# Running sum of key features: adding DMAs into DRAM from GpSimd's queue in place of VectorE additions in SBUF

## The chip, the cores and the metric

The kernel runs on one core of one Trainium2 chip. A core has five engines with a queue of instructions each: TensorE (PE) for matrix products, VectorE (DVE) and ScalarE (ACT) for element-wise work, GpSimd (POOL) for element-wise work beside them, and SyncE (SP), which here issues the transfers between DRAM and the core's memory (SBUF). Engines work in parallel and in the order of their own queue; they wait for each other through semaphores. The metric is the time of one execution on the device in microseconds, as the median of several runs.

## The reference, cut to what matters

The input `x` (2048 tokens of 1024 features) is normalised; an attention block A and a gated block B are computed of it, and the result is `x + A * silu(B)`. The change touches only a part of A:

```python
qkv = (x @ wqkv) ...                       # 32 heads of 32 features
pk = einsum("bhsd,hdf->bhsf", k, w_phi)
phi_k = concat([softmax(pk), softmax(-pk)], -1)     # 64 features per head and token
kv = einsum("bhsf,bhsd->bhfd", phi_k, v)   # sum over tokens
z  = einsum("bhsf->bhf", phi_k)            # sum over tokens
num = einsum("bhqf,bhfd->bhqd", phi_q, kv)
den = einsum("bhqf,bhf->bhq", phi_q, z) + 1e-6
o = num / den
```

`z`, the sum of the key features over all 2048 tokens, is what is accumulated in another way.

## The kernel before, in words

**Matrix products.** Large products are done by Strassen-like recombination into seven block products, named B11, T2, T3, B21, T1, T4 and B22. Each float32 operand is split into a high and a low part (`split`: line 130 on ScalarE makes the high part, line 131 on VectorE the low part), and `mm3` (lines 135 to 137) makes three matmuls of the parts. Several block products share a PSUM bank: B21 adds on top of B11, T4 on top of T3, B22 on top of T1, and between the two the bank is read into SBUF ("evacuated"). For the gated block these evacuations are line 1069 (B11, ScalarE), 1071 (T2), 1073 (T3), and 1079 to 1088 for the blocks that end a result; line 1089 multiplies a gate on GpSimd. In this stage one block is 4 x 3 = 12 matmuls.

**Stages.** The tokens are handled in two chunks of 1024. For each chunk come the projections V, K and Q, then the products with the gate and up weights (28 units of 7 blocks). After both chunks come the product with the down weights and the attention's second half. During chunk 0's gated stage and all of chunk 1, side work is mixed in as "background" tasks, one at a time: `background(anchor)` issues the next task from a list, to follow a given instruction. In chunk 1's gated stage one is issued every six blocks, and a second list (weight sums on GpSimd, `wd_sums`, lines 571 to 578) every fourteen.

**The task of the change.** `k_task(hb, t)` handles one tile of 128 tokens and one half `hb` of the heads: 16 tiles for each of two halves, 32 tasks. It loads raw keys and values (lines 463 and 464), makes the features (`features`, lines 446 to 454: maxima and minima, two subtractions at lines 449 and 450 that write the buffer `e_k`, the exponential at line 451 on ScalarE, sums and reciprocals), scales `e_k` in place (line 467), splits `e_k` and the values for TensorE (lines 130 and 131), and adds `e_k` (128 x 1024, 512 KB) to `zacc` (line 474 copies in the first tile, line 476 adds in the others). `e_k` is one buffer, slot 53, which all tasks use in turn; `zacc` is slot 54. The products of the task's features and values (line 486) are issued on TensorE with the next background task.

After the 16 tiles of a half, three more tasks follow: `kv_sum` and `kv_blocks`, which put the products together, and `z_broadcast` (line 521 on), which splits `zacc`, multiplies it by a matrix of ones so that each partition has the sum over all 128, and stores that to DRAM (`zb_d`).

**What sets the order.** Outside the first and last stages the order of each engine's queue is made at build time by a scheduler that simulates the program and places every instruction where it thinks it is ready; the anchors bound it from one side. Nothing reorders on the chip: an instruction that waits holds its engine's queue. SP issues nearly every transfer, among them the weight loads `w<-ws_d` (line 388), up to eight 512 KB slots ahead of their use. GpSimd issues none.

Of the kernel before, what the change touches and what calls it, by code (L numbers as in the profile page):

```python
# [10 lines left out]
F32 = mybir.dt.float32  # L11
F32R = mybir.dt.float32r
AF = mybir.ActivationFunctionType
ALU = mybir.AluOpType
# [4 lines left out]
P = 128  # L19
# [8 lines left out]
HB = 512  # L28
# [21 lines left out]
def hedgehog_glu_kernel(  # L50
# [12 lines left out]
    nc = tc.nc  # L63
# [4 lines left out]
    dram = ctx.enter_context(tc.tile_pool(name="dram", bufs=1, space=DRAM))  # L68
# [9 lines left out]
    xo_d = dram.tile([7, P, 4, HB], F32, name="xo_d")  # L78
    e_d = dram.tile([TT, 2, P, 2 * HB], F32, name="e_d")
    r_d = dram.tile([CTT, 2, P, 32], F32, name="r_d")  # L80
    zb_d = dram.tile([2, P, 2 * HB], F32, name="zb_d")
    kvbd_d = dram.tile([2, P, 2 * HB], F32, name="kvbd_d")
    ws_d = dram.tile([2 * NJ, 4, P, 2 * HB], F32, name="ws_d")
# [30 lines left out]
    def whole(i):  # L114
        return slots[i].rearrange("p a n -> p (a n)")
# [4 lines left out]
    def run(i, n):  # L120

        name, k = where[i]
        return blocks[name][0][:, k:k + n]

    def pair(i):
        return slots[i][:, 0], slots[i][:, 1]

    def split(o, src):

        nc.scalar.copy(o[0], src)  # L130
        return nc.vector.tensor_sub(o[1], src, o[0].bitcast(F32))  # L131
# [308 lines left out]
    def features(name, p, e):  # L440

        nh = HB // DH
        st = small.tile([P, 4, nh], F32, name=f"st{name}", tag="st", bufs=2)
        pv = p.rearrange("p (h d) -> p h d", d=DH)
        mx, mn = st[:, 0], st[:, 1]
        nc.vector.tensor_reduce(mx, pv, axis=AX.X, op=ALU.max)
        nc.vector.tensor_reduce(mn, pv, axis=AX.X, op=ALU.min)
        ev = e.rearrange("p (h t d) -> p h t d", t=2, d=DH)
        nc.vector.tensor_tensor(ev[:, :, 0], pv, mx[:, :, None].to_broadcast([P, nh, DH]), op=ALU.subtract)  # L449
        nc.vector.tensor_tensor(ev[:, :, 1], mn[:, :, None].to_broadcast([P, nh, DH]), pv, op=ALU.subtract)  # L450
        nc.scalar.activation(e, e, AF.Exp)  # L451
        s2, r2 = [st[:, a:a + 2].rearrange("p t h -> p (t h)") for a in (2, 0)]
        nc.vector.tensor_reduce(s2, e.rearrange("p (g d) -> p g d", d=DH), axis=AX.X, op=ALU.add)  # L453
        nc.vector.reciprocal(r2, s2)
        return r2
# [3 lines left out]
    e_k, zacc = whole(53), whole(54)  # L459
    kvb = banks[4:]  # L460

    def k_task(hb, t):
        nc.sync.dma_start(kraw, qkv_d[K, t, hb])
        nc.sync.dma_start(vraw, qkv_d[V, t, hb])
        r = features(f"k{t}{hb}", kraw, e_k)
        e3 = e_k.rearrange("p (g d) -> p g d", d=DH)
        nc.vector.tensor_mul(e3, e3, r[:, :, None].to_broadcast([P, 32, DH]))  # L467

        ph, v = [o.rearrange("p (g a f) -> p g a f", g=8, a=2)
                 for o in (run(36, 2).rearrange("p a b n -> p (a b n)"), whole(38))]  # L470
        split((ph[:, :, 0], ph[:, :, 1]), e_k.rearrange("p (g f) -> p g f", g=8))
        split((v[:, :, 0], v[:, :, 1]), vraw.rearrange("p (g f) -> p g f", g=8))
        if t == 0:
            nc.vector.tensor_copy(zacc, e_k)
        else:
            nc.vector.tensor_add(zacc, zacc, e_k)
        kv_due.append((t, ph, v))

    kv_due = deque()
# [40 lines left out]

    def z_broadcast(hb):

        for i in range(2):
            z = zacc[:, i * HB:(i + 1) * HB]
            a = pair(38)
            split(a, z)
            nc.tensor.matmul(kvb[i], ones, a[0], start=True, stop=False)
            nc.tensor.matmul(kvb[i], ones, a[1], start=False, stop=True)
            nc.scalar.copy(z, kvb[i])
        nc.sync.dma_start(zb_d[hb], zacc)  # L530
# [469 lines left out]
    for hb in range(2):  # L1000
        bg.extend([lambda hb=hb, t=t: k_task(hb, t) for t in range(TT)])
        bg.extend([lambda hb=hb, f=f: f(hb) for f in (kv_sum, kv_blocks, z_broadcast)])
# [162 lines left out]
    for n, (i, j, cs) in enumerate(dsteps):  # L1165
# [24 lines left out]
        if n and n * 32 // 78 > (n - 1) * 32 // 78 and late:  # L1190
            t, hb = late.pop(0)
# [193 lines left out]
```

## Time and profile before

| what | value |
|---|---|
| runs | 2380.21, 2378.32, 2374.84 us; median 2378.32 us |
| profiled execution, first to last instruction | 2376.2 us; the page gives no time outside it |
| TensorE busy | 2361.1 us (99%), granted clock 1.000 |
| VectorE busy | 1778.2 us (75%) |
| ScalarE busy | 1022.0 us (43%) |
| GpSimd busy | 959.8 us (40%) |
| DMA | 600.49 MB, mean 253 GB/s |

The page lists busy time by engine, a picture of the span in 40 slices, DMA queues, the chain of work that ended last, and groups of instructions by line with their count, busy time, mean duration and the idle time ahead of them on their engine. "L476" is line 476 of the kernel. Tiles are shown by name without number: `fc` is the block of slots that holds `e_k`, `zacc` and the raw keys and values, `p` holds split operands, `w` the split weights, `bank` a PSUM bank. "a <- b" means a is written from b. A wait "X <- Y" says that X's engine sat idle until Y was done. Busy time off the engine that bounds the kernel costs nothing by itself.

### The profile page before, as it was taken

What the parts mean: (1) busy time and instruction counts of PE and PEld (TensorE: products, weight loads), DVE (VectorE), ACT (ScalarE), POOL (GpSimd) and SP (SyncE); (2) the same over time, 40 slices, a digit from 0 to 9 for tenths busy, and PEclk for the clock granted to TensorE, in tenths of its full rate; (3) what the DMA queues carried; (4) which work ended last, traced back from release to release, by engine and by line L of the source; (5) the groups of instructions that cost most, each with busy time, mean ns of one, the idle gap of its engine ahead of it and who ended that gap; (6) DMA issues with size and microseconds to landing.
All of it is one profiled execution on the core that took longest, in us unless ns stands there. A gap on an engine that the chain in (4) does not pass through costs nothing.

```text
span 2376.2 us, 31871 instructions
## 1 busy us (share of the span) xinstructions
PE 2361.1 (99%) x10972; PEld 1966.2 (83%) x10972; DVE 1778.2 (75%) x2340; ACT 1022.0 (43%) x1516; POOL 959.8 (40%) x613
## 2 busy tenths in 40 slices
PE   9999999999999999999999999999999999999999
PEld 8888888888888888888878888888888888888887
DVE  8626777877777575668884888865889998878776
ACT  7333344444434342324443444444444334455553
POOL 0223456666666433123443222232333334424566
PEclk9999999999999999999999999999999999999999
DMA  6689987778776787677777666668666666876665
GB/s 237 234 310 321 339 318 263 289 265 291 259 283 246 248 309 261 234 262 242 275 266 250 231 219 216 222 207 312 209 220 230 239 218 209 288 252 244 204 209 177
DMA packets 233587, 600.49 MB, mean 253 GB/s; under 512 B 30672, under 2 KB 30928, under 8 KB 228816
## 3 DMA queue, kind: packets, MB, share of 16 engines
q1 hardware_dynamic: 233424, 598.45, 72.3%
q8 instruction: 86, 1.41, 0.2%
q14 instruction: 77, 0.63, 0.1%
HBM read 363.20 MB, written 235.14 MB: 252 GB/s over the span
## 4 chain that ended last, share of the span: by engine, by line
PE 92%; DVE 4%; DMA 2%; issue 1%; ACT 1%; POOL 0%; SPq 0%; DVEq 0%; ACTq 0%
PE bank L135 29%; PE bank L137 29%; PE bank L136 29%; PE bank L696 1%; PE bank L672 1%; PE bank L486 1%; PE bank L285 1%; DMA fc<-wqkT 1%; DVE p L131 1%; DVE w L131 0%; DVE fc L450 0%; DVE fc L449 0%; DMA x<-x 0%; DMA fa<-wf_d 0%; DVE stk L453 0%
## 5 line engine op out<-in xcount | busy, mean ns | idle before, releaser
L136 PE MATMUL bank<-x,w 128*128 128x512 f32 x2352 | 915.7, 389 | 0.0
L135 PE MATMUL bank<-x,w 128*128 128x512 f32 x2352 | 909.8, 390 | 1.6 <-DVE fc L1073 1.1
L137 PE MATMUL bank<-x,w 128*128 128x512 f32 x2352 | 906.3, 390 | 0.0
L130 ACT CAST w<-fa 128x512 fp32r<-128x512 f32 (+1 forms) x430 | 294.8, 688 | 574.0 <-PE bank L136 365.9
L135 PEld LDWEIGHTS bank<-x,w 128*128 128x128 f32 x2352 | 441.6, 188 | 94.1 <-DVE fc L1073 2.3
L137 PEld LDWEIGHTS bank<-x,w 128*128 128x128 f32 x2352 | 441.5, 188 | 91.5 <-DVE w L131 0.4
L136 PEld LDWEIGHTS bank<-x,w 128*128 128x128 f32 x2352 | 441.6, 188 | 90.3
L131 DVE TENSOR_TENSOR w<-fa,w 128x512 fp32r<-128x512 f32 (+1 forms) x430 | 415.8, 972 | 104.1 <-ACT w L130 90.8
L135 PE MATMUL bank<-w,x 128*128 128x512 f32 x708 | 277.8, 393 | 0.2 <-ACT w L877 0.2
L136 PE MATMUL bank<-w,x 128*128 128x512 f32 x708 | 276.2, 390 | 0.9 <-DVE w L878 0.9
L137 PE MATMUL bank<-w,x 128*128 128x512 f32 x708 | 275.8, 390 | 0.0
L1089 POOL TENSOR_TENSOR fb<-fb,fc 128x512 f32<-128x512 f32 x57 | 89.0, 1561 | 291.6 <-DVE fc L1088 264.8
L137 PEld LDWEIGHTS bank<-w,x 128*128 128x128 f32 x708 | 132.9, 188 | 27.8 <-DVE x L868 0.3
L136 PEld LDWEIGHTS bank<-w,x 128*128 128x128 f32 x708 | 133.1, 188 | 27.4 <-DVE w L878 1.3
L135 PEld LDWEIGHTS bank<-w,x 128*128 128x128 f32 x708 | 133.1, 188 | 27.2 <-ACT w L877 0.6
L628 POOL TENSOR_TENSOR fc<-fc 128x1024 f32<-128x1024 f32 x32 | 81.4, 2542 | 173.7 <-ACT fc L451 125.4
L1088 DVE TENSOR_TENSOR fc<-fc,bank 128x512 f32<-128x512 f32 x84 | 57.5, 684 | 102.5 <-PE bank L137 97.4
L131 DVE TENSOR_TENSOR x<-fa,x 128x512 fp32r<-128x512 f32 x112 | 113.5, 1013 | 23.8 <-ACT x L130 23.6
L130 ACT CAST w<-fb 128x512 fp32r<-128x512 f32 x112 | 69.7, 622 | 141.7 <-PE bank L136 115.3
L131 DVE TENSOR_TENSOR p<-fc,p 128x1024 fp32r<-128x1024 f32 (+2 forms) x97 | 103.9, 1081 | 10.6 <-ACT p L130 8.3
L130 ACT CAST p<-fc 128x1024 fp32r<-128x1024 f32 (+2 forms) x97 | 70.7, 738 | 90.3 <-DVE fc L467 50.7
L640 POOL TENSOR_TENSOR fc<-fc,sa 128x1024 f32<-128x1024 f32 x32 | 70.4, 2199 | 90.6 <-DVE sa L637 90.6
(258 smaller groups left out, 3231.2 us busy)
## 6 DMA issues: line engine op xcount, KB each, us to landing
ws_d<-w SPq DMA_DIRECT2D x112, 512.0 KB, 4.2
w<-ws_d SPq DMA_DIRECT2D x112, 512.0 KB, 4.8
fa<-w_gu SPq DMA_DIRECT2D x84, 512.0 KB, 4.4
fa<-h_d SPq DMA_DIRECT2D x84, 512.0 KB, 4.0
fa<-wf_d SPq DMA_DIRECT2D x32, 1024.0 KB, 6.9
h_d<-fc SPq DMA_DIRECT2D x120, 256.0 KB, 3.2
fc<-e_d SPq DMA_DIRECT2D x48, 512.0 KB, 4.8
fc<-qkv_d SPq DMA_DIRECT2D x80, 256.0 KB, 4.3
```

The source lines that it names most:

```text
L130: nc.scalar.copy(o[0], src)
L131: return nc.vector.tensor_sub(o[1], src, o[0].bitcast(F32))
L135: nc.tensor.matmul(o, a[0], b[0], start=first, stop=False, **kw)
L136: nc.tensor.matmul(o, a[0], b[1], start=False, stop=False, **kw)
L137: nc.tensor.matmul(o, a[1], b[0], start=False, stop=last, **kw)
L285: nc.tensor.matmul(ps[:, gs], r[:, gs], bd[:, 4 * f + g], start=True, stop=True)
L486: nc.tensor.matmul(kvb[g // 2][:, g % 2 * 256:g % 2 * 256 + 256], v[:, g].rearrange("p a f -> p (a f)"), ph[:, g].rearrange("p a f -> p (a ...
L628: nc.gpsimd.tensor_mul(ez, e, zb)
L640: nc.gpsimd.tensor_mul(e3, e3, r2[:, :, None].to_broadcast([P, 32, DH]))
L672: nc.tensor.transpose(ps[:, j * P:(j + 1) * P], e[:, k * P:(k + 1) * P], ident)
L1088: v = nc.vector.tensor_add(b, u2 if q == 3 else u1, bank)
L1089: nc.gpsimd.tensor_mul(g, g, b)
```

## The change

The running sum is kept in a new DRAM buffer `zs_d`, one part for each half of the heads. The first tile's task writes `e_k` there with a transfer issued from GpSimd's queue; the other fifteen issue a transfer that adds `e_k` to what is there. VectorE's copy and additions go. `z_broadcast` first loads the sum from `zs_d` into `zacc` by a transfer on SP's queue, and goes on as before. The arithmetic is the same. Since two further lines stand in the file, lines behind them move by one or two.

```diff
+    zs_d = dram.tile([2, P, 2 * HB], F32, name="zs_d")
     zb_d = dram.tile([2, P, 2 * HB], F32, name="zb_d")
...
         split((ph[:, :, 0], ph[:, :, 1]), e_k.rearrange("p (g f) -> p g f", g=8))
         split((v[:, :, 0], v[:, :, 1]), vraw.rearrange("p (g f) -> p g f", g=8))
         if t == 0:
-            nc.vector.tensor_copy(zacc, e_k)
+            nc.gpsimd.dma_start(zs_d[hb], e_k)
         else:
-            nc.vector.tensor_add(zacc, zacc, e_k)
+            nc.gpsimd.dma_start(zs_d[hb], e_k, accum_op=ALU.add)
         kv_due.append((t, ph, v))
...
     def z_broadcast(hb):
 
+        nc.sync.dma_start(zacc, zs_d[hb])
         for i in range(2):
             z = zacc[:, i * HB:(i + 1) * HB]
```

## The prediction

> **What bounds the kernel now.** I read the page's totals first, then busy time by stage, then TensorE's waits in the stage that the change touches.
>
> ```profile
> span 2376.2 us, 31871 instructions
> PE 2361.1 (99%) x10972; PEld 1966.2 (83%) x10972; DVE 1778.2 (75%) x2340; ACT 1022.0 (43%) x1516; POOL 959.8 (40%) x613
> ```
> ```profile
> 320.00:740.00 420.00, 420.00 (x1861) 347.55 (x1860) 326.91 (x437) 185.43 (x271) 261.26 (x178) 1.00 0.76 272
> ...
> 890.00:1300.00 410.00, 406.57 (x1853) 337.72 (x1852) 286.90 (x337) 152.83 (x200) 131.31 (x85) 1.00 0.75 257
> 1300.00:1600.00 300.00, 299.77 (x1383) 249.93 (x1382) 234.88 (x292) 135.05 (x174) 85.03 (x56) 1.00 0.65 219
> ```
> ```profile
> PE bank L486 <- DVE p L131: 2.1, 2, 1.2
> PE bank L135 <- DVE fc L1073: 1.1, 2, 0.9
> PE bank L135 <- DVE fb L1081: 0.4, 1, 0.4
> ```
> The columns of the second view are stretch, length, and busy time of PE, PEld, DVE, ACT and POOL, then the granted clock and the DMA share. TensorE is the bound all through. The running sum is built between about 887 and 1577 us, so the stretches 890 to 1300 and 1300 to 1600 hold it. There TensorE is idle 3.43 + 0.23 = 3.66 us in all at clock 1.00, and the third view (TensorE's waits from 890 to 1600) puts 3.6 us of that on VectorE. So nothing done to VectorE here can win more than 3.7 us, or 0.15%.
>
> **What is removed.**
>
> ```profile
> L474 DVE COPY fc<-fc x2: 686/686/686, 889.3 to 1317.5; 128x1024 f32<-128x1024 f32 x2
> L476 DVE TENSOR_TENSOR fc<-fc x30: 1214/1224/2312, 908.2 to 1575.8; 128x1024 f32<-128x1024 f32 x30
> L476 DVE TENSOR_TENSOR fc<-fc 128x1024 f32<-128x1024 f32 x30 | 43.9, 1462 | 0.5
> ```
> Two copies (1.4 us) and thirty additions (43.9 us) leave VectorE, which is 73% busy in this window ((286.90 + 234.88) / 710). Most of that lies beside TensorE's work. It is on the path where the chain of waits runs through it:
>
> ```profile
> 1234.02 1.21 DVE fc L476
> 1236.14 2.32 DVE p L131
> 1238.50 1.21 PE bank L486 x8
> ```
> Here the addition stands ahead of the split (L131) that the k-v products (L486) wait for. The two L486 waits, 2.1 us, are of this kind and I take them as won. The other 1.5 us hang on evacuations that the addition does not precede, and stay. Gain: 2.1 us, with 0 and 3.7 as its ends.
>
> **What is added, and the new wait.** (Line numbers are those of the kernel before.) Each of the 32 tasks now issues a 512 KB transfer from GpSimd out of `e_k`, 30 of them adding into DRAM. `e_k` is one buffer. In the changed program the next task's L449 (the first write of `e_k`) waits for that transfer's completion. Before, the reader was VectorE itself and no wait was needed. The question is therefore T, the time from the end of L467 (`e_k` complete) to the transfer's completion, against the gap that the order leaves until the next L449. One of the tightest gaps:
>
> ```profile
> 1473.26 1.21 DVE L453 TENSOR_REDUCE stk<-fc 128x32 f32<-128x1024 f32 x1
> 1474.38 0.67 DVE L1073 TENSOR_TENSOR fc<-fc,bank 128x512 f32<-128x512 f32 x1
> ...
> 1475.35 1.22 DVE L467 TENSOR_TENSOR fc<-fc,stk 128x1024 f32<-128x1024 f32 x1
> 1476.61 1.22 DVE L476 TENSOR_TENSOR fc<-fc 128x1024 f32<-128x1024 f32 x1
> 1477.76 1.23 DVE L131 TENSOR_TENSOR p<-fc,p 128x1024 fp32r<-128x1024 f32 x1
> 1478.90 0.68 DVE L1081 TENSOR_TENSOR fb<-fc,bank 128x512 f32<-128x512 f32 x1
> ...
> 1481.88 0.68 DVE L449 TENSOR_TENSOR fc<-fc,stk 128x512 f32<-128x512 f32 x1
> ```
> 1481.88 - 1476.57 = 5.3 us. There are 31 such gaps in the window; the first and the last are
>
> ```profile
> 886.44 1.23 DVE L467 TENSOR_TENSOR fc<-fc,stk 128x1024 f32<-128x1024 f32 x1
> ...
> 901.04 0.68 DVE L449 TENSOR_TENSOR fc<-fc,stk 128x512 f32<-128x512 f32 x1
> ...
> 1559.63 1.23 DVE L467 TENSOR_TENSOR fc<-fc,stk 128x1024 f32<-128x1024 f32 x1
> ...
> 1567.55 0.69 DVE L449 TENSOR_TENSOR fc<-fc,stk 128x512 f32<-128x512 f32 x1
> ```
> 13.4 and 6.7 us. Sorted, in us: 5.3, 5.3, 6.4, 6.5, 6.6, 6.6, 6.7, 6.7, 7.4, 7.4, 7.6, 7.6, 8.2, 8.7, 8.9, 9.1, 9.1, 9.1, and then thirteen of 12.4 or more. The changed order keeps L449 at its place but for one split in front of it here and there.
>
> *How long T is.* No transfer leaves GpSimd's queue in this trace, and none adds. The nearest rows:
>
> ```profile
> ws_d<-w SPq DMA_DIRECT2D x112, 512.0 KB, 4.2
> w<-ws_d SPq DMA_DIRECT2D x112, 512.0 KB, 4.8
> ...
> wo_d<-p SPq DMA_DIRECT2D x21, 512.0 KB, 6.8
> ```
> ```profile
> L1089 POOL TENSOR_TENSOR fb<-fb,fc 128x512 f32<-128x512 f32 x25 | 35.3, 1412 | 212.5 <-DVE fc L1088 212.5
> L576 POOL TENSOR_TENSOR fb<-fb 128x512 f32<-128x512 f32 x12 | 22.2, 1846 | 1.4 <-DMA fb<-w_down 0.6
> ```
> Landing: a plain store of this size takes 4.2 us, the lower end. An adding store must fetch its target before it can write, so I take a load and a store one after the other, 4.8 + 4.2 = 9.0 us. The high end is two transfers of the slowest kind, 13.6 us. GpSimd's queue is in order: it is 30% busy here ((131.31 + 85.03) / 710) with instructions of 1.4 to 1.8 us, so the issue waits on average 0.3 x 1.6 = 0.5 us, between 0 and 1.8. What issuing costs GpSimd itself is unseen: not below zero, and I set it near a short GpSimd instruction, 1.3 us, at most 1.8. T = 9.0 + 0.5 + 1.3 = 10.8 us, ends 4.2 and 17.2; the ends are far apart and I stay near the load-and-store row because the addition needs both accesses.
>
> By the Trainium skill (DMA: Bandwidth & Descriptors, Anatomy of one DMA — SWDGE (gpsimd) path) a transfer from GpSimd takes about 2.0 us plus bytes / 436e3, an estimate of 3.2 us for 512 KB; with that T is shorter than every gap and the sum is rival one's. The rows above (4.2 to 6.8 us for plain transfers of this size, on a busy chip) do not bear this out here.
>
> *What TensorE feels.* Behind L449 on VectorE stand L450, the exponential on ScalarE that L453 waits for, and behind L453 the evacuation L1073 of a T3 block (1473.26 and 1474.38 in the timeline above). The next block but one (T4) adds into T3's bank, so TensorE goes on only when L1073 is done; one block lies between. Its length:
>
> ```profile
> 1363.21 0.39 PE L137 MATMUL bank<-x,w 128*128 128x512 f32 x1
> 1363.44 0.39 PE L135 MATMUL bank<-x,w 128*128 128x512 f32 x1
> ```
> 0.226 us from one matmul to the next, times 12, is 2.7 us; less the evacuation's own 0.67 us that leaves 2.0 us. So each task stalls TensorE by about T - gap - 2.0 us. With T = 10.8 the 18 short gaps enter, 14 of them with a remainder, and their sum is 26.4 us. The same sum by T: 0 at 7.3 and below, 1.4 at 8, 5.9 at 9, 16.0 at 10, 47.0 at 12, 83 at 14, 110 at 15.4.
>
> *Other additions.* TensorE's order hardly moves. SP gets two loads of the sum (zs_d, 512 KB each) ahead of the broadcast; they are issued three task slots after the last addition, the blocks that use them keep their places in TensorE's order, so I count 0, and 2 x 4.8 = 9.6 us if that cover is gone. The weight loads (ws_d) stand behind each of them in SP's queue and would wait too if the last addition were late. GpSimd holds its queue while it waits for `e_k` or the previous addition; behind it stand the gate products L1089, whose own wait for VectorE (212.5 us idle before them) shows room, 0. Traffic grows by 32 x 512 KB written, 30 read again, 2 read back: 34 MB on
>
> ```profile
> q1 hardware_dynamic: 233424, 598.45, 72.3%
> ```
> 598 MB. In this window the DMA share is 0.75 and 0.65, so it fits; 0.
>
> **Sum.** 2376.2 (span) - 2.1 + 26.4 = 2400.5 us. The page shows nothing outside the span, and the median of the runs, 2378.32, is 2.1 us above it, so I put the runs' median at 2402 us, 1.0% slower.
>
> **Rivals.**
>
> *One: the transfer hides.* If T stays under 8 us, the sum of stalls is at most 1.4 us and the gain at most 3.7, so the time lies between 2374.6 and 2379.7: no change. For it: the plain store lands in 4.2 us, and 13 gaps are above 12 us anyway. Against: 18 gaps under 9.1 us, and two memory accesses in series.
>
> *Two: the adding transfer is much slower, T of 13 us and more.* Then each further microsecond of T costs 18 us (18 short gaps), and the long ones begin to enter at T = 14.4 (12.4 + 2.0): with 83 us at 14 the runs' median is 2378.3 - 2.1 + 83 = 2459, with 110 us at 15.4 it is 2486. For it: 512 KB took 6.8 us in one group, and GpSimd's and VectorE's reads hold each other up (L476 goes from 1.21 to 2.31 us), which could delay the issue. By the Trainium skill (SBUF — State Buffer, Who interferes with whom) GpSimd cannot write a transfer's descriptors while VectorE runs a copy in its two-port mode; the only VectorE copies in this window are L474's two, which the change removes, so that rule adds nothing here.
>
> *Three: faster.* VectorE loses 45.3 us of work, and if T is under every gap the three waits of 3.6 us all go. It decides below T = 7.3. It gives 2378.3 - 3.7 = 2374.6 us, which is still within 0.2%. To pass that bound it would need idle time that TensorE does not have.
>
> **Chances.** 0.2% of 2378 is 4.8 us, about what a measurement of this kernel can tell from no change. T between 8.8 (stalls of about 5 us) and 13: 0.46, the forecast, own range 2380 to 2442. Rival two: 0.22. Rival one, with T from 8 to 8.8 added: 0.28. Faster by over 0.2%: 0.04. So slower 0.68, same 0.28, faster 0.04. The range runs from 2374 (full gain, no stall) to 2460 (T = 14); above it I leave 0.12, below it 0.04.
>
> **What would show it.** Right: L476 and L474 gone from VectorE; waits of VectorE at L449 named after a transfer to zs_d, in the short-gap tasks alone; TensorE's idle time between 890 and 1600 up from 3.7 to some 28 us, behind L1073 or L1088; landing of zs_d near 9 us. Wrong: landing of 5 us or less and no L449 wait (rival one); landing of 11 us or more, with the tasks at long gaps waiting too (rival two); GpSimd rows of many us per issue, or L486 waiting for L131 in task after task, which would mean that the products' place in TensorE's order was the tight one and not the evacuation; lost time outside 890 to 1600 us, which none of the steps gives.

## The result and the profile after

The changed kernel takes 2381.91 us (median of 20 runs, 2375.61 to 2384.87), the kernel before 2377.41 us in the runs taken beside it: a ratio of 1.0017, with an interval of 1.001 to 1.0024. That is 4 us slower (0.0017 x 2377); the interval leaves 1 out, but the change is within the 0.2% taken as none. The forecast was 2402 us.

The profiled execution took 2381.26 us, 1.8 us of them outside the span. In the changed file lines up to `z_broadcast` stand one further down than before, those behind it two: the first write of `e_k` is now L450 (L449 before), its completion L468 (L467), the adding transfer L477, the evacuations L1071, L1073 and L1075. In the kernels of the experiments they can stand one or two further.

From the page of the kernel after, the totals and the DMA queues (packets, MB, share of 16 engines' span):

```profile
span 2379.5 us, 31909 instructions
PE 2362.4 (99%) x10972; PEld 1965.2 (83%) x10972; DVE 1747.7 (73%) x2308; ACT 1018.3 (43%) x1514; POOL 982.8 (41%) x645
...
q1 hardware_dynamic: 233712, 599.49, 72.8%
q0 software_dynamic: 4608, 16.78, 4.2%
```

VectorE lost 32 instructions and 30.5 us of busy time (45.3 us were taken off it, so its other instructions took some 15 us longer), and 32 transfers with 16.78 MB appear on a queue of their own. The span is only 3.3 us longer. Busy time by stretch after (columns as in the prediction):

```profile
740.00:890.00 150.00, 148.98 (x657) 122.49 (x656) 102.46 (x111) 60.02 (x78) 65.64 (x42) 1.00 0.78 269
890.00:1300.00 410.00, 404.80 (x1839) 334.50 (x1838) 275.20 (x319) 149.40 (x198) 143.45 (x100) 1.00 0.87 275
1300.00:1600.00 300.00, 298.28 (x1371) 248.01 (x1370) 215.80 (x274) 133.92 (x173) 96.23 (x72) 1.00 0.81 244
```

TensorE is idle 1.02 + 5.20 + 1.72 = 7.9 us from 740 to 1600, where it was idle 3.7 us before: 4.3 us more, about what the times differ by. Of this, 1.0 us lies from 740 to 890, ahead of the tasks' waits; the kernels below lose 0 to 1.1 us there too (e6 aside), so a difference of 1 us between two profiles says little. TensorE's waits in the three stretches, then VectorE's wait for the transfer and the rows of all that writes or reads `zs_d` (for the issues on GpSimd the duration min/median/max in ns), all of the kernel after:

```profile
PE bank L136 <- ACT fc L1071: 3.4, 3, 1.7
PE bank L136 <- DVE fc L1087: 1.2, 1, 1.2
PE bank L487 <- DVE p L132: 1.0, 2, 0.7
PE bank L136 <- DVE fb L1083: 1.0, 2, 0.8
PE bank L136 <- ACT fb L1081: 0.9, 2, 0.6
PE bank L136 <- ACT fb L423: 0.4, 1, 0.4
```
```profile
L477 POOL DMA_DIRECT2D zs_d<-fc x30: 862/879/902, 908.6 to 1580.0; - x30
L475 POOL DMA_DIRECT2D zs_d<-fc x2: 606/672/738, 885.6 to 1317.7; - x2
...
  DVE fc L450: 27.4, 15
...
DMA to landing us min/median/max: 3.7/7.2/9.7
```

The last row takes in the two plain stores and the two loads; the 30 adding transfers alone land in 5.4, 7.5 and 9.7 us (least, median, most), counted from the start of their issue.

So the new wait exists, at the place predicted: in 15 of the 32 tasks VectorE stood at L450 for the transfer, 27.4 us in all. Only a part of that reached TensorE, and by another way than predicted. One such task in order of time, VectorE first, then ScalarE, GpSimd and TensorE (start, duration, engine, line; in brackets the idle time before it and its releaser):

```profile
1476.12 1.22 DVE L468 TENSOR_TENSOR fc<-fc,stk 128x1024 f32<-128x1024 f32 x1
...
1486.68 0.69 DVE L450 TENSOR_TENSOR fc<-fc,stk 128x512 f32<-128x512 f32 x1 [3.95 <-DMA zs_d<-fc]
1487.29 0.69 DVE L451 TENSOR_TENSOR fc<-stk,fc 128x512 f32<-128x512 f32 x1
```
```profile
1488.04 1.28 ACT L452 ACT_TABLE_LOAD   x1 [4.94 <-DVE fc L451]
1489.34 1.06 ACT L452 ACTIVATE fc<-fc 128x1024 f32<-128x1024 f32 x1
1490.30 0.60 ACT L131 CAST w<-fa 128x512 fp32r<-128x512 f32 x1
1490.81 0.58 ACT L1071 COPY fc<-bank 128x512 f32<-128x512 f32 x1
```
```profile
1477.97 0.87 POOL L477 DMA_DIRECT2D zs_d<-fc  x1 [4.42 <-issue]
```
```profile
1491.44 0.50 PE L136 MATMUL bank<-x,w 128*128 128x512 f32 x1 [0.58 <-ACT fc L1071]
```

`e_k` was complete at 1477.34 and L450 ran at 1486.68: T is 9.3 us here. VectorE waits 3.95 us, the exponential (L452) is late by it, and behind the exponential in ScalarE's queue stands B11's evacuation (L1071), which TensorE's B21 block waits for. Of 3.95 us on VectorE 0.58 us are left on TensorE.

### The profile page after: what moved, and what is told of

Its sections match the earlier page's. It is cut to its first block, busy times and chain, and to the rows that moved or that the text cites. A ratio compares the mean times of both kernels' runs of the same rounds, so it can differ in the third digit from the quotient of the medians.

```text
span 2379.5 us, 31909 instructions
## 1 busy us (share of the span) xinstructions
PE 2362.4 (99%) x10972; PEld 1965.2 (83%) x10972; DVE 1747.7 (73%) x2308; ACT 1018.3 (43%) x1514; POOL 982.8 (41%) x645
## 3 DMA queue, kind: packets, MB, share of 16 engines
q0 software_dynamic: 4608, 16.78, 4.2%
## 5 line engine op out<-in xcount | busy, mean ns | idle before, releaser
L131 ACT CAST w<-fa 128x512 fp32r<-128x512 f32 (+1 forms) x430 | 294.7, 688 | 547.9 <-PE bank L137 337.8
L132 DVE TENSOR_TENSOR w<-fa,w 128x512 fp32r<-128x512 f32 (+1 forms) x430 | 420.1, 982 | 114.9 <-ACT w L131 101.4
L477 POOL DMA_DIRECT2D zs_d<-fc x30 | 26.4, 881 | 275.2 <-issue 94.1
L131 ACT CAST w<-fb 128x512 fp32r<-128x512 f32 x112 | 69.7, 622 | 142.9 <-PE bank L137 111.8
L132 DVE TENSOR_TENSOR x<-fa,x 128x512 fp32r<-128x512 f32 x112 | 111.5, 996 | 23.4 <-ACT x L131 23.2
L132 DVE TENSOR_TENSOR p<-fc,p 128x1024 fp32r<-128x1024 f32 (+2 forms) x97 | 109.7, 1140 | 20.2 <-ACT p L131 18.0
L131 ACT CAST p<-fc 128x1024 fp32r<-128x1024 f32 (+2 forms) x97 | 70.7, 737 | 105.3 <-DVE fc L468 58.9
```

Of the source, the lines that this page charges most:

```text
L477: nc.gpsimd.dma_start(zs_d[hb], e_k, accum_op=ALU.add)
```

## The experiments

Every ratio is against the kernel before, run beside it. The table sets TensorE's idle time from 740 to 1600 us in one profile of each kernel (stretch length less busy time, three stretches) beside it; the wait column is VectorE's idle time for the sum's transfers at the first write of `e_k` in a task. (`kv_sum`, which writes `e_k` after each half, waits for them too: 1.3 us after, 4.6 in e5, 6.6 in e9, 8.6 in e4.)

| kernel | VectorE's additions | transfers | `e_k` | wait, us | PE idle, us | ratio |
|---|---|---|---|---|---|---|
| before | yes | none | one | 0 | 3.7 | 1 |
| after | no | adding | one | 27.4 | 7.9 | 1.0017 [1.001, 1.0024] |
| e1_two_buffers | no | adding | two | 0 | 3.1 | 0.9997 [0.9988, 1.0006] |
| e1_again (the same) | no | adding | two | 0 | 3.8 | 0.9998 [0.9989, 1.0006] |
| e12_two_plain | no | plain | two | 0 | 1.1 | 0.9979 [0.9971, 0.9988] |
| e2_plain | no | plain | one | 5.1 | 1.1 | 0.9981 [0.9972, 0.999] |
| e3_no_sum | no | none | one | 0 | 1.4 | 0.9981 [0.9973, 0.999] |
| e7_zacc_traffic | yes | adding, out of `zacc` | one | 0 | 4.8 | 0.9998 [0.9989, 1.0007] |
| e14_zacc_plain | yes | plain, out of `zacc` | one | 0 | 2.6 | 0.9995 [0.9986, 1.0004] |
| e5_both | yes | adding | one | 25.8 | 15.6 | 1.0062 [1.005, 1.0074] |
| e9_parallel | no | two adding, two targets | one | 91.8 | 35.4 | 1.0227 [1.0212, 1.0241] |
| e4_two_adds | no | adding, twice | one | 137.7 | 60.5 | 1.0511 [1.0495, 1.0528] |

**Is it the wait?** A second `e_k` takes away what makes L450 wait, and leaves all else.

```diff
     def k_task(hb, t):
+        e_k = whole(53 + t % 2)
```

> The changed kernel with e_k in two buffers in turn (slots 53 and 54; slot 54 is idle until the broadcast), so that no task writes a buffer that the transfer of the task before still reads. Transfers, their size and their number stay. Theory A (the loss is VectorE's wait at the first write of e_k for a transfer that takes 8.4 us from the end of L468): the 27.4 us of waits go, TensorE's idle time between 890 and 1600 us falls from 6.9 to 3.7 us or less, and the time is 0 to 3 us under the kernel before (ratio 0.9987 to 1.0000). Theory B (the loss is the added traffic: DMA share 0.75 to 0.87, weight loads 4.8 to 5.7 us to landing): the wait goes but TensorE's idle time stays near 6.9 us and the ratio near 1.0017.

Measured: 2376.49 us, against 2381.91 us with one buffer. The wait at L450 is gone, and TensorE's idle time falls from 7.9 to 3.1 us. E1's stretches, its waits of TensorE from 740 to 1640, and the wait of VectorE behind the longest of them:

```profile
740.00:890.00 150.00, 149.65 (x661) 123.59 (x660) 102.39 (x111) 59.95 (x78) 65.21 (x42) 1.00 0.79 269
890.00:1300.00 410.00, 407.50 (x1859) 339.15 (x1859) 266.91 (x321) 154.29 (x203) 148.03 (x103) 1.00 0.86 278
1300.00:1600.00 300.00, 299.77 (x1385) 250.29 (x1385) 219.23 (x283) 139.15 (x183) 92.66 (x70) 1.00 0.82 250
```
```profile
PE bank L136 <- DVE fc L1084: 2.3, 1, 2.3
```
```profile
DVE fc L1084 <- DMA h_d<-fc: 4.0, 1, 4.0
```

The kernel was run again beside the ones below:

> e1_two_buffers once more beside e12_two_plain on the same chip, for the difference of the two: both theories ratio 0.9997 within 0.0010.

It gave 2376.3 us, 0.9998. The wait therefore costs some 5 us (1.0017 less 0.9997 or 0.9998, 0.2% of 2377), or 4.1 to 4.8 us of idle TensorE. The second buffer also changes the order of some queues a little; that this isn't what wins shows below, where plain transfers with one buffer and with two (e2 and e12) come out alike, 0.9981 and 0.9979. The kernel without it is level with before, not faster.

**What is VectorE's relief worth?** Neither VectorE nor a transfer adds here; only the first tile of each half is stored.

```diff
         else:
-            nc.gpsimd.dma_start(zs_d[hb], e_k, accum_op=ALU.add)
+            pass
```

> The changed kernel without the 30 adding transfers and without additions on VectorE (the sum over tiles is left out; only the first tile's is written): what relieving VectorE alone is worth. Both theories: no wait at L450, the three waits of 3.6 us on VectorE partly gone: 0 to 3.7 us under the kernel before (ratio 0.9985 to 1.0000). Against e1_two_buffers it gives the price of the transfers without their wait: 0 by theory A, 3 to 4 us by theory B.

Measured: 2374.15 us, 0.9981 [0.9973, 0.999]. TensorE's idle time falls by 2.3 us, from 3.7 to 1.4. So relief alone wins between 2.4 and 6.4 us by the interval; the profile bears out 2.3 of it.

**What does the adding kind of transfer cost?** The same bytes are written, plainly, so that each tile overwrites the last, in the same order of instructions on all five queues as the kernel after.

```diff
-            nc.gpsimd.dma_start(zs_d[hb], e_k, accum_op=ALU.add)
+            nc.gpsimd.dma_start(zs_d[hb], e_k)
```

> The changed kernel with plain writes in place of the 30 adding transfers (same queue, source, size and waits; each overwrites the last, so the sum over tiles is left out). The two plain transfers of the changed kernel landed in 3.9 us, the adding ones in 7.2. Theory A (wait): e_k is free about 4.8 us after L468, under every gap; no wait at L450, TensorE idle in 890 to 1600 us at most 3 us, ratio 0.998 to 1.000. Theory B (the number of transfers and their issue on GpSimd cost by themselves): ratio stays at 1.001 or above.

Measured: 2373.33 us, 0.9981 [0.9972, 0.999]. Plain transfers land in 4.1 us, VectorE waits 5.1 us in all for them, and TensorE's idle time is 1.1 us: the whole of the loss is gone with the adding. Against the kernel after that is 6.8 us of idle TensorE and 8.6 us of time. What is left open is how much of the difference is the wait and how much the load; the plain write with two buffers, in the order of e1, tells them apart.

```diff
+        e_k = whole(53 + t % 2)
...
-            nc.gpsimd.dma_start(zs_d[hb], e_k, accum_op=ALU.add)
+            nc.gpsimd.dma_start(zs_d[hb], e_k)
```

> The two buffers of e1_two_buffers with plain writes in place of the adding transfers (sum over tiles left out). Every engine's queue has the same instructions in the same order as in e1_two_buffers, and neither waits for a transfer at L450, so the difference is what the adding kind costs through the load on the DMA engines alone (adding: 7.2 us to land and 4.1% of the 16 engines' span; plain: about 4 us and 2.0%). Theory A (only the wait costs): the same as e1_two_buffers, ratio 0.9997 within 0.0010. Theory B (the load costs 3 to 4 us): ratio 0.998, as e2_plain and e3_no_sum.

Measured: 2372.48 us, 0.9979 [0.9971, 0.9988], 0.19% below e1, in which nothing waits for the sum's transfers either. E12's stretches, its queue of these transfers, its row in the list of DMA issues (KB, median us to landing), and the two waits that answer to those of e1:

```profile
740.00:890.00 150.00, 150.00 (x665) 124.17 (x664) 103.00 (x113) 60.57 (x79) 66.51 (x42) 1.00 0.78 272
890.00:1300.00 410.00, 409.10 (x1868) 340.67 (x1867) 266.50 (x323) 154.77 (x203) 141.45 (x103) 1.00 0.81 279
1300.00:1600.00 300.00, 299.77 (x1386) 250.35 (x1385) 217.73 (x283) 138.84 (x183) 88.10 (x70) 1.00 0.74 250
```
```profile
q0 software_dynamic: 4608, 16.78, 2.0%
```
```profile
zs_d<-fc POOLq DMA_DIRECT2D x32, 512.0 KB, 4.3
```
```profile
PE bank L136 <- DVE fc L1084: 0.9, 1, 0.9
```
```profile
DVE fc L1084 <- DMA h_d<-fc: 2.4, 1, 2.4
```

By this pair of times the adding load costs 4 us beside the wait. Of the 2.0 to 2.7 us that the idle time shows of it, 1.4 us are one place: VectorE's write at L1084 (L1083 after) waits for a store (`h_d<-fc`) to have read its buffer, 4.0 us with adding transfers beside it and 2.4 us with plain ones, and TensorE waits 2.3 us instead of 0.9. The rest is spread over waits below half a microsecond and isn't assigned.

**The adding load on the kernel before.** VectorE's sum stays; the transfers go out of `zacc`, and nothing reads what they leave in DRAM.

```diff
         if t == 0:
             nc.vector.tensor_copy(zacc, e_k)
+            nc.gpsimd.dma_start(zs_d[hb], zacc)
         else:
             nc.vector.tensor_add(zacc, zacc, e_k)
+            nc.gpsimd.dma_start(zs_d[hb], zacc, accum_op=ALU.add)
```

> The kernel before, additions on VectorE kept, plus 32 transfers from GpSimd of the same size and kind (30 adding), out of zacc after each addition, into a DRAM buffer that nothing reads. zacc is written again only some 15 us later, so nothing should wait for them, and they are spread over the stage as in the changed kernel (those of e6_traffic all ran between 809 and 1000 us). Theory A: no wait of VectorE for zs_d worth a microsecond; ratio 1.000 to 1.001. Theory B (traffic as such costs 2 to 4 us, as e3_no_sum against e1_two_buffers hints): ratio 1.001 to 1.002.

> e7_zacc_traffic (additions on VectorE kept, transfers out of zacc that nothing waits for) with plain writes in place of the adding ones; every engine's queue has the same instructions in the same order as in e7_zacc_traffic. If the load of the adding kind costs 4 to 5 us whatever VectorE does, as e1_two_buffers against e12_two_plain shows for the relieved VectorE: ratio 0.998, under the kernel before although nothing was taken off VectorE. If that price belongs to the order and the buffers of e1_two_buffers alone: the same as e7_zacc_traffic, 0.9998 within 0.0010.

Measured: 2375.8 us, 0.9998 [0.9989, 1.0007] with adding, 2375.52 us, 0.9995 [0.9986, 1.0004] with plain transfers in the same order (on another chip, beside its own runs of the kernel before). The times show no price of adding here, where e1 against e12 showed 0.19%. The profiles show one: TensorE idle 4.8 against 2.6 us, a difference of 2.2 us, as in e1 against e12 (2.0 to 2.7). The intervals of all four ratios are about 0.1% to each side, so a price of 2 us (0.1%) fits both pairs, 4 us only the one. I take 2 us as shown by the profiles, with one execution of each, and leave open whether it is more where VectorE is relieved.

An earlier form of this control sent an idle buffer instead of `zacc`:

```diff
+            nc.gpsimd.dma_start(zs_d[hb], whole(16).bitcast(F32))
...
+            nc.gpsimd.dma_start(zs_d[hb], whole(16).bitcast(F32), accum_op=ALU.add)
```

> The kernel before, additions on VectorE kept, and beside them the same 32 transfers from GpSimd (2 plain, 30 adding, 512 KB each, to a DRAM buffer that nothing reads), but out of a tile of the operand B11 that nobody writes in this stage: the traffic and GpSimd's issue without the wait on e_k. Theory A: ratio 1.000 (0.9995 to 1.0005), TensorE idle 3.7 us in 890 to 1600. Theory B: ratio 1.0015 to 1.002, weight loads land in 5.7 us.

It measured 2389.65 us, 1.0053 [1.0041, 1.0066], but isn't the control that was meant. The rows of its transfers and of its longest TensorE wait:

```profile
L479 POOL DMA_DIRECT2D zs_d<-x x30: 853/878/1403, 815.6 to 993.9; - x30
```
```profile
PE bank L136 <- DVE fc L417: 4.3, 1, 4.3
```

A transfer that waits for nothing was placed early: all 30 went out within 180 us, instead of the 670 us of the kernel after, and TensorE lost 5.5 us between 740 and 890 us. Bunched, the same number of transfers went with a longer time than spread (e7, 0.9998); the order of the queues differs too, and what caused the waits was not followed further. Of the change it tells nothing.

**How the loss grows with T.** One kernel issues the adding transfer twice, the second behind the first; another adds to a second target, so that the two need not wait for each other.

```diff
             nc.gpsimd.dma_start(zs_d[hb], e_k, accum_op=ALU.add)
+            nc.gpsimd.dma_start(zs_d[hb], e_k, accum_op=ALU.add)
```

> The changed kernel with the adding transfer issued twice in each task, the second waiting for the first (the sum is then counted twice, so the output differs): the time from L468 to the release of e_k grows from 8.4 to about 16 us. Theory A, with the stall per task as in the prediction (T - gap - 2.0 us): 60 to 130 us more than the kernel before (ratio 1.025 to 1.055), waits in the tasks with long gaps too. Theory B: twice the traffic, twice the loss: 8 us (ratio 1.0035).

```diff
             nc.gpsimd.dma_start(zs_d[hb], e_k)
+            nc.gpsimd.dma_start(zt_d[hb], e_k)
         else:
             nc.gpsimd.dma_start(zs_d[hb], e_k, accum_op=ALU.add)
+            nc.gpsimd.dma_start(zt_d[hb], e_k, accum_op=ALU.add)
```

> The changed kernel with a second adding transfer per task into a second DRAM buffer, which need not wait for the first: e_k is released by the later of the two, at T of about 10.5 to 12 us by my estimate. The prediction's formula (T - gap - 2.0 us, gaps of the kernel before) gives 16 us at T = 10, 26 at 10.8, 47 at 12, so theory A expects 14 to 47 us more than before (ratio 1.006 to 1.020). Theory B (twice the traffic): 8 us, ratio 1.0035.

Measured: 2497.94 us, 1.0511, and 2431.72 us, 1.0227. VectorE's wait for the transfers and the stretches of e4, then the same of e9 (where L451 is the first write of `e_k`):

```profile
DVE fc L450 <- DMA zs_d<-fc: 137.7, 24, 10.3
```
```profile
890.00:1300.00 410.00, 388.00 (x1705) 318.93 (x1703) 237.24 (x287) 129.26 (x164) 142.99 (x104) 0.96 0.88 270
1300.00:1600.00 300.00, 262.47 (x1122) 211.50 (x1120) 178.78 (x232) 110.28 (x150) 90.64 (x72) 0.94 0.79 226
```
```profile
DVE fc L451 <- DMA zt_d<-fc: 91.8, 21, 9.3
```
```profile
890.00:1300.00 410.00, 393.57 (x1765) 324.66 (x1764) 252.54 (x311) 141.47 (x187) 153.93 (x114) 0.98 0.91 285
1300.00:1600.00 300.00, 281.19 (x1249) 230.43 (x1248) 189.37 (x247) 116.60 (x151) 93.42 (x76) 0.97 0.85 250
```

In the tasks that waited, T (from `e_k` complete to its next write) had a median of 8.5 us after, 11.8 us in e9 and 15.6 us in e4. Against the 2376 us of the kernel that doesn't wait (e1), they lose 5.5, 55 and 122 us. The loss isn't all idle time: the granted clock falls too, to 0.98 and 0.97 in e9 and 0.96 and 0.94 in e4. By an estimate from these rows (busy time times the missing share of the clock) e4 loses some 388 x 0.04 + 262 x 0.06 = 31 us to the clock alone in these two stretches, e9 some 394 x 0.02 + 281 x 0.03 = 16 us.

**The wait without the relief.** VectorE keeps its additions and the adding transfers go out of `e_k` beside them.

```diff
         if t == 0:
+            nc.vector.tensor_copy(zacc, e_k)
             nc.gpsimd.dma_start(zs_d[hb], e_k)
         else:
             nc.gpsimd.dma_start(zs_d[hb], e_k, accum_op=ALU.add)
+            nc.vector.tensor_add(zacc, zacc, e_k)
...
-        nc.sync.dma_start(zacc, zs_d[hb])
```

> The changed kernel's transfers out of the single e_k, with VectorE's additions kept beside them (into zacc, as before): the new wait without the relief of VectorE. Theory A: the wait at the first write of e_k stays, up to 1.2 us shorter per task since the addition now fills part of it; time at or above the changed kernel: ratio 1.0015 to 1.004. If the relief is worth what e3_no_sum says (4.5 us) and the wait is not much shorter: 1.003 to 1.004.

Measured: 2393.4 us, 1.0062 [1.005, 1.0074]. VectorE's waits and the longer stretch:

```profile
DVE fc L450 <- DMA zs_d<-fc: 25.8, 9, 5.0
DVE fc L500 <- DMA zs_d<-fc: 4.6, 1, 4.6
```
```profile
890.00:1300.00 410.00, 399.37 (x1802) 329.94 (x1802) 281.07 (x331) 149.66 (x196) 140.87 (x99) 0.99 0.84 270
```

VectorE waits about as long in sum as in the kernel after (25.8 against 27.4 us), in fewer and longer pieces, and TensorE loses 11.9 us of idle time against before (15.6 less 3.7) instead of 4.3. The lengths of the pieces go far to explain it: less the prediction's cover of 2.0 us each, wait by wait, e5's leave 9.4 us and those after 5.3 us, and e5 has the wait of `kv_sum` (L500) besides. Whether VectorE's relief is worth more beside the wait than alone is therefore not shown by this pair.

**Another way to relieve VectorE.** GpSimd does the addition itself, with no transfer.

```diff
-            nc.vector.tensor_add(zacc, zacc, e_k)
+            nc.gpsimd.tensor_add(zacc, zacc, e_k)
```

> The kernel before with the 30 additions of e_k to zacc on GpSimd in place of VectorE, no transfers. A GpSimd instruction on 128 x 1024 takes 2.2 to 2.5 us here, so e_k is free about 3 us after L468, under every gap. Theory A: no wait at L449 over 1 us and VectorE relieved as in e3_no_sum (ratio 0.9981): ratio 0.998 to 1.000, a version faster than both. Against it: GpSimd and VectorE hold each other up (L476 from 1.21 to 2.31 us), which could give the gain back: ratio 1.000 to 1.002.

Measured: 2380.69 us, 1.0015 [1.0006, 1.0025]: slower, with 43.9 us less work on VectorE. From 890 to 1600, the low parts (L131) of the kernel before, then of e10, and e10's addition:

```profile
L131 DVE TENSOR_TENSOR w<-fa,w 128x512 fp32r<-128x512 f32 (+1 forms) x111 | 104.6, 944 | 24.8 <-ACT w L130 22.7 <-DMA qkv_d<-fb 1.8
L131 DVE TENSOR_TENSOR p<-fc,p 128x1024 fp32r<-128x1024 f32 (+2 forms) x69 | 81.2, 1182 | 0.2
```
```profile
L131 DVE TENSOR_TENSOR w<-fa,w 128x512 fp32r<-128x512 f32 (+1 forms) x111 | 130.3, 1175 | 23.4 <-ACT w L130 23.1
L131 DVE TENSOR_TENSOR p<-fc,p 128x1024 fp32r<-128x1024 f32 (+2 forms) x69 | 102.4, 1489 | 9.9 <-ACT p L130 9.9
L476 POOL TENSOR_TENSOR fc<-fc 128x1024 f32<-128x1024 f32 x30 | 74.3, 2477 | 245.8 <-DVE fc L467 245.8
```

These two groups grew by 25.7 + 21.2 = 46.9 us, more than the 43.9 us taken off. The Trainium skill (SBUF — State Buffer, Who interferes with whom) says that a VectorE instruction with two SBUF inputs contends with a GpSimd instruction that reads SBUF; these rows agree. The adding transfer, which holds GpSimd for its issue alone (0.88 us), does relieve VectorE, though not of all: its busy time after is 275.20 + 215.80 = 491.0 us where it was 521.8, 30.8 us less where 43.9 us of additions and a copy of 0.7 us went from these stretches. Low parts (L131, L132 after) are longer here too: those of 128x1024 in `p` take 1666 ns on average against 1492.

## Why the prediction was wrong, point by point

**The bound and the gain: right.** TensorE bounds the kernel, and VectorE's 45 us could win only a few microseconds of it. The term of 2.1 us is borne out by the idle time, 2.3 us less in e3 and 2.6 us less in e2. The times of e2, e3 and e12 are 4.5 to 5 us below before; the prediction's ceiling of 3.7 us lies within their intervals. The L486 waits that were to be won are gone in e2, e3 and e12; after, 1.0 us of them is back (L487 for L132).

**The wait at the next write of `e_k`: right.** It appears in 15 tasks, where 18 gaps were counted as short and 14 with a remainder; the tasks of long gaps don't wait, and a second buffer removes it.

**T: this step failed.** The prediction took 9.0 us to land (a load and a store in series), 0.5 us in GpSimd's queue and 1.3 us for the issue: 10.8 us. Measured: GpSimd starts 0.6 us behind L468 (1477.97 against 1477.34 in the task above), and an adding transfer lands in 7.5 us at the median, between the plain transfer (4.2 us for the same 30 in e2) and the sum of two. The issue is no term of its own: the profile counts the landing from the issue's start. In the task above it gives 8.6 us, and 1477.97 + 8.6 is 1486.6, where L450 starts, so the 0.87 us of the issue lie within. The sum thus had the landing 1.5 us too long and counted the issue twice. 0.6 + 7.5 is 8.1 us; in the tasks that waited, whose transfers are the slower ones, T is 7.5 to 10.4 us, 8.5 at the median (8.46; the expectations call it 8.4). The forecast hung on it: the prediction's own sum of stalls is 26.4 us at T = 10.8 and about 2.5 us at 8.5, so with T right it would have said no change (2.1 us won, 2.5 lost).

**The stalls from T: the size about right, the way only in part.** With the waits that were measured, less 2.0 us each, the prediction's formula gives 5.3 us; the wait measured 5 us in time and 4.1 to 4.8 us in idle TensorE. That the sums meet is in part luck, for in single tasks they don't: the task above gives 1.95 us by the formula and cost TensorE 0.58; the one whose L450 ran at 1243.03 after a wait of 2.33 us gives 0.33, and TensorE lost 1.68 us behind its exponential. By T alone the formula gives about 43 us at 11.8 against 55 in e9, and about 115 at 15.6 against 122 in e4. In these two it overstates the idle time (about 32 and 57 us more than e1's in the table, and in e4 the last tasks lie behind 1600) and leaves out the clock, which makes up for it. The path named was VectorE's evacuation L1073, with one block of cover. The longest group after is L1071, on ScalarE behind the exponential (3.4 us, three times); the prediction counted VectorE's queue and passed over what stands behind the exponential in ScalarE's.

**Traffic at 0: wrong by about 2 us in the profiles; by 4 in one pair of times, by nothing that shows in the other.** The prediction counted bytes against a DMA share of 0.75. The adding transfers use 4.2% of the engines' span for the bytes that plain ones move in 2.0%, and the stage's share went from 0.75 and 0.65 to 0.87 and 0.81. The weight loads land later. After, from the list of DMA issues (4.8 us before):

```profile
w<-ws_d SPq DMA_DIRECT2D x112, 512.0 KB, 5.7
```

TensorE doesn't wait for them in the rows above. Where a wait could be followed (L1084 in e1), it was for a store that held a buffer.

**GpSimd's queue and the loads of the sum at 0: right.** No wait of TensorE in the rows after names GpSimd's gate products or the two loads of `zs_d`. ScalarE does wait for the loads, 8.3 us in two pieces (at 1260 and 1591 us), but TensorE isn't idle behind the first (no wait between 1249 and 1357 us) and loses next to nothing behind the second. Behind 1600 us, to 2368, TensorE is idle 0.25 + 1.12 us after and 0.95 us before: the loss lies where the tasks are.

**The rivals.** The change landed where rival one put it (no change), with less of its mechanism: it had T under 8 us and stalls of at most 1.4 us, and the gain of up to 3.7 us ahead of them. (The chances put T from 8 to 8.8 with it.) In fact T is 8.5 us, and the wait (5 us) and the load (2 to 4 us) together outweigh the relief (2.3 to 5 us) by 4 us. That 2381.91 us falls just inside the 2380 to 2442 us set for T from 8.8 to 13 is luck: T is shorter, and a load that was put at 0 makes up for it. The page that spoke for it, the Trainium skill (DMA: Bandwidth & Descriptors, Anatomy of one DMA — SWDGE (gpsimd) path), gives an estimate of 3.2 us; the plain transfers of this queue take about 1 us more (4.1 and 4.3 us in e2 and e12), and the adding ones more than twice as long (7.5 us).

## What to carry to other kernels

Where a transfer takes the place of an engine's instruction, its source buffer is held until the transfer lands: compare its landing time, with what the queue ahead of the issue adds, with the gap to the buffer's next write, task by task, and give it a second buffer if they are near (here that was worth 0.2%). An adding transfer is to be priced as nearly two plain ones, in time to land and in DMA engine time. And relief of an engine that isn't the bound is worth only the bound's idle time behind it: 45 us of VectorE were worth 2 to 5 us here, and the adding transfers cost 7 to 9 (after against e2).

## What was not expected of the hardware

- An adding transfer of 512 KB lands in 7.5 us (6.3 out of `zacc` in e7) where a plain one of the same queue takes 4.1 to 4.3, less than a load and a store in series (9.0), and takes twice the DMA engines' time (4.2% against 2.0% of their span for the 32).
- The granted clock falls where TensorE has idle gaps of a few microseconds: to 0.96 and 0.94 in e4, whose longest wait of TensorE is 6.3 us, and to 0.98 and 0.97 in e9. The Trainium skill (TensorE: Matmul & The Clock Gate, Part 1) says that the clock halves after an idle window of about 3.4 us; means between 0.94 and 1 agree with a halved clock for a small part of the time, though no row here shows a single window.
- Thirty additions moved to GpSimd, 74.3 us there, came with VectorE's other instructions taking 46.9 us longer: no relief at all.
